# Forty small swap DMAs, a row load of D, and moved buffers in a one-core SSM convolution with an MLP

## The chip, the cores and the metric

The kernel runs on one core of a Trainium2 chip. The metric is the device time of one execution in microseconds (us); the median of the timed runs is compared.

## The reference

Two residual blocks over x of shape 2048 x 640 (bf16). Block A is a gated long convolution: a four-tap causal shift of k, times v, convolved along the sequence with one 2048-tap filter per channel, plus a skip term D. Block B is a Mish MLP of width 1728.

```python
x = A_q
h = x + A_ref(layernorm(x), A_k, A_v, A_shift_k, A_ssm_k, A_ssm_D)
h2 = h + B_ref(layernorm(h), B_w1, B_b1, B_w2)

def A_ref(q, k, v, shift_k, ssm_k, ssm_D):
    kv = causal_shift(k, shift_k) * v            # 4 taps per channel
    y = irfft(rfft(pad(kv)) * rfft(pad(ssm_k)))  # convolution over 2048 steps
    return q * (y + kv * ssm_D)
def B_ref(x, w1, b1, w2):
    h = x @ w1 + b1
    return (h * tanh(softplus(h))) @ w2
```

## The kernel before, in words

The convolution is done as a transform in two matmul stages, a product, and an inverse in two stages. The 640 channels are five blocks of 128 (`dc`), in two groups: group 0 is dc 0 to 2 (96 channel groups of the array `KP`), group 1 is dc 3 and 4 (64).

- **Filter side.** `dadd` adds D to the first filter tap (DVE, L458), `k1pe` transposes the filter (PE, L466), `s1kpe` is stage 1 (PE, L409 and L410), `s2kpe` stage 2 with the table G (PE, L438). The spectrum lands in `KP`.
- **Swap.** The product of complex numbers needs `KP` with its upper and lower 64 partitions exchanged. `swap` copies it to `KPS` by DMA within SBUF (L564): one DMA for each half of each group, four in all.
- **Signal side.** `ktpe` transposes k (L491), `kspe` applies the taps as 76 small matmuls for each dc (L514), `kv` multiplies by v (DVE, L525), then stage 1 (`s1vpe`) and stage 2 (`s2vpe`, L438). ACT evicts stage 2 into a ring `xa`; `prod` multiplies it into `KP` and `KPS` (DVE, L637).
- **Inverse and MLP.** `i1pe` (L648, L649), then for each of 16 row tiles: `i2pe` (L687), the gate `wb` (DVE, L699), the residual `h` (L703), LayerNorm statistics (L708), the scaling `dr` (L717), a transpose `trpe` (L724), the MLP matmuls `m1pe` (L743) and `m2pe` (L759), and the last addition `res` (L768). LayerNorm of x (`ln1`, L596) runs in between.

Evictions out of PSUM have one line for each engine: L316 is ACT, L318 is DVE. PSUM has four double banks (`PS`) in the convolution.

All big arrays are views into one SBUF tile, `arena`, at offsets written out by hand, and share space over time. `KPS` lies over the filter and over k, so it may be written once both have been read. Its part for group 1 also holds `kvb3` and `kvb4`, the kv blocks of dc 3 and 4 (`OFF_KVB2`), so the second swap is issued after `s1vpe3` and `s1vpe4`.

The order on each engine comes from `_schedule`, a list planner in Python with costs and priorities written into the `OP` calls. Each engine then runs its list in order and waits on semaphores. All loads, swaps and stores are issued from SP's queue; the loads of D and of the constants from ACT's; the taps and b1 from POOL's. Eight semaphores serve the DMAs of SP's and ACT's queues in turn, so a DMA is issued once the one eight places ahead of it has landed.

Of the kernel before, what the change touches and what calls it, by code (L numbers as in the profile page):

```python
# [40 lines left out]
OFF_KVB2 = OFF_KPS + 24576  # L41
# [196 lines left out]
def kernel(  # L238
# [90 lines left out]
    Dn = small.tile([P, NDC], BF16, name="Dn")  # L329
# [19 lines left out]
    OP("warm", ("act", 0.2), w=["dumm"], emit=emit_warm, prio=-1)
    def emit_consts(e):  # L350
        nc.scalar.dma_start(consts[:], dram["consts"])
        nc.scalar.dma_start(Dn[:], A_ssm_D.rearrange("(c p) -> p c", p=P))
# [148 lines left out]
    def shift_s(dc, prio):  # L501
# [4 lines left out]
        def ks(e):  # L506
            kvb.tile = view([P, 64, 16, 2], OFF_KVB + dc * 4096 if dc < 3 else OFF_KVB2 + (dc - 3) * 4096)
            outs = [ps_alloc(x).rearrange("p (i t d) -> p i t d", i=2, t=16) for x in rts]
            for src in range(-3, 16):
# [7 lines left out]
                after=wr + ([o for o in ops if o.name.startswith("ktpe")] if dc >= 3 else []))  # L517
# [75 lines left out]
    for t2 in range(16):  # L593
        def fn(e, t2=t2):
            for hh in range(2):
                nc.vector.bn_stats(st1[:, t2, hh, :], xn_t()[:, t2, hh * 320:(hh + 1) * 320])  # L596
            nc.vector.bn_aggr(mv1[:, t2, :], st1[:, t2, :, :])
        OP(f"ln1_{t2}", ("dve", 1.1), r=[("x", t2)], w=[("mv1", t2)], emit=fn, prio=58 if t2 < 4 else CHAIN[t2])
    for lo, hi in ((0, 4), (4, 8), (8, 12), (12, 16)):
        OP(f"ln1s{lo}", ("pool", 1.0), r=[("mv1", t) for t in range(lo, hi)] + ["mhalf"], w=[("r1", t) for t in range(lo, hi)], prio=45,  # L600
           emit=lambda e, lo=lo, hi=hi: rsqrt_eps(r1v[:, lo:hi], mv1[:, lo:hi, 1], hi - lo))

        def ln1f_emit(e, lo=lo, hi=hi):
            nc.vector.scalar_tensor_tensor(nmr1[:, lo:hi], mv1[:, lo:hi, 0], -1.0, r1v[:, lo:hi], ALU.mult, ALU.mult)
        OP(f"ln1f{lo}", ("dve", 0.2), r=[("r1", t) for t in range(lo, hi)], w=[("nmr1", t) for t in range(lo, hi)], emit=ln1f_emit, prio=45)
# [3 lines left out]
    for grp in range(2):  # L609
# [3 lines left out]
        for ci in range(len(ch)):  # L613
            xa = _RT(R_XA, f"xa{grp}_{ci}")
            s1k_pes = [x for x in ops if x.name.startswith("s1kpe")] if (grp, ci) == (0, 0) else []
            rt, o, f0, nf = s2_pe("s2v", grp, ci, lambda grp=grp: B_t[grp]("bvs"), f"bvs{grp}", 25 + grp * 10, xa, s1k_pes)
# [61 lines left out]
    ks_pes = [o for o in ops if o.name.startswith("kspe")]
    for t2 in range(16):
# [38 lines left out]
        o_dr = OP(f"dr{t2}", ("dve", 0.42), r=[("x", t2), ("mv2", t2), ("r2", t2)], allocs=[hc], emit=drf, prio=pr, after=ks_pes)  # L718
# [95 lines left out]
```

## Time and profile before

| | us |
|---|---|
| median of 3 runs | 272.43 (272.22 to 274.0) |
| the profiled execution, its own time | 271.45 |
| span of its instructions | 269.5 |
| PE busy | 223.9 (83%) |
| DVE busy | 155.0 (58%) |
| ACT busy | 138.9 (52%) |

The profiled execution took 1.95 us more than its span, and 0.98 us less than the median of the runs. Busy shares are a mean over stages that differ: the convolution is the first 125 us, and the MLP with its LayerNorms the rest.

### The profile page before, as it was taken

The numbers are of one execution on the slowest core, as the hardware profiler recorded it, in microseconds if no ns is written. First come the engines' busy times: TensorE is split into PE (matmuls) and PEld (weight loads), VectorE is DVE, ScalarE is ACT, GpSimd is POOL, SyncE is SP. The second block draws the span as 40 slices with busy tenths as digits, with TensorE's granted clock in tenths as the row PEclk, the third lists the DMA queues.
The fourth block names the chain that finished last, engine by engine and source line by source line (L and its number), as shares of the span: only waits on it lengthen the run. The fifth ranks groups of instructions, "written<-read, shape, count | busy, mean of one in ns | idle before, by whom it ended". The sixth has DMA issues, their size and how long they took to land.

```text
span 269.5 us, 6850 instructions
## 1 busy us (share of the span) xinstructions
PE 223.9 (83%) x3018; PEld 169.1 (63%) x3024; DVE 155.0 (58%) x300; ACT 138.9 (52%) x192; POOL 22.6 (8%) x56
## 2 busy tenths in 40 slices
PE   2069799885097597894899999999999999999994
PEld 2059788774086497792788774755577557744672
DVE  0038889888069976998899988813862101210121
ACT  2028699284079976975587297445711460056200
POOL 5000000000000000021231132200220000000000
PEclk9999999999569979998699999999999999999999
DMA  6999900029945199960000000010001000100011
GB/s 235 319 416 418 419 19 2 6 61 215 196 150 246 41 202 259 398 233 2 1 2 24 11 18 2 0 49 4 0 24 51 24 0 27 49 24 2 1 47 49
DMA packets 8285, 28.63 MB, mean 106 GB/s; under 512 B 1408, under 2 KB 5312, under 8 KB 6592
## 3 DMA queue, kind: packets, MB, share of 16 engines
q1 hardware_dynamic: 7344, 28.02, 31.4%
q8 instruction: 23, 0.38, 0.6%
q10 hardware_dynamic: 800, 0.17, 0.5%
q0 software_dynamic: 112, 0.01, 0.1%
q14 instruction: 6, 0.05, 0.1%
HBM read 20.33 MB, written 2.62 MB: 85 GB/s over the span
## 4 chain that ended last, share of the span: by engine, by line
PE 57%; DVE 18%; DMA 10%; issue 6%; ACT 5%; POOL 2%; ACTq 0%; DVEq 0%; SPq 0%; POOLq 0%
PE banks L759 23%; PE banks L743 19%; DVE arena L318 6%; DMA Dn<-in_A_ssm_D_dram 5%; DVE arena L637 4%; ACT arena L316 4%; DMA arena<-arena 4%; PE banks L409 4%; DVE st L596 3%; DVE arena L525 3%; PE banks L466 2%; PE banks L438 2%; PE banks L687 2%; PE banks L514 2%; PE banks L724 2%
## 5 line engine op out<-in xcount | busy, mean ns | idle before, releaser
L316 ACT CAST arena<-banks 128x1024 bf16<-128x1024 f32 (+3 forms) x76 | 69.5, 1003 | 27.4 <-PE banks L410 20.8
L749 ACT ACTIVATE arena<-banks,b1s 128x512 bf16<-128x512 f32 (+2 forms) x84 | 43.9, 548 | 46.7 <-PE banks L743 45.5
L743 PE MATMUL banks<-arena 128*128 128x512 bf16 (+2 forms) x414 | 64.4, 311 | 0.9 <-DVE arena L318 0.6
L759 PE MATMUL banks<-arena 128*128 128x320 bf16 x448 | 62.3, 299 | 0.0
L759 PEld LDWEIGHTS <-arena 128*128 128x128 bf16 x448 | 43.6, 98 | 16.8
L743 PEld LDWEIGHTS <-arena 128*128 128x128 bf16 x420 | 36.6, 100 | 24.7 <-issue 0.7
L768 DVE TENSOR_TENSOR arena<-banks,arena 128x640 bf16<-128x640 f32 x16 | 13.1, 818 | 58.7 <-PE banks L759 58.7
L318 DVE CAST arena<-banks 128x1024 bf16<-128x1024 f32 (+1 forms) x28 | 32.8, 1203 | 6.5 <-PE banks L410 4.2
L438 PE MATMUL banks<-arena 128*128 128x64 bf16 (+1 forms) x512 | 23.8, 204 | 5.3 <-ACT arena L316 2.7
L409 PE MATMUL banks<-consts,arena 128*64 128x128 bf16 x320 | 24.7, 234 | 2.3 <-ACT arena L316 1.2
L410 PE MATMUL banks<-consts,arena 128*64 128x128 bf16 x320 | 25.2, 236 | 1.4 <-issue 1.4
L438 PEld LDWEIGHTS <-arena 128*128 128x128 bf16 x512 | 21.4, 101 | 7.6 <-issue 6.7
L637 DVE TENSOR_TENSOR arena<-arena 128x960 bf16<-128x960 bf16 (+2 forms) x42 | 24.4, 661 | 2.5 <-DMA arena<-arena 2.2
L316 ACT COPY arena<-banks 128x1024 bf16<-128x1024 bf16 (+1 forms) x14 | 11.6, 852 | 26.1 <-PE banks L466 15.0
L410 PEld LDWEIGHTS <-arena 128*64 128x64 bf16 x320 | 21.1, 120 | 3.7 <-issue 3.4
L409 PEld LDWEIGHTS <-arena 128*64 128x64 bf16 x320 | 21.6, 120 | 2.5 <-issue 1.5
L648 PE MATMUL banks<-consts,arena 128*128 128x128 bf16 x160 | 19.1, 220 | 2.1 <-DVE arena L637 1.8
L694 ACT ACTIVATE arena<-arena,nmr,r1v 128x640 bf16<-128x640 bf16 x16 | 14.6, 926 | 10.5 <-DVE arena L703 10.2
L466 PE MATMUL banks<-consts,arena 128*128 128x128 bf16 x80 | 7.4, 262 | 14.5 <-DVE arena L458 9.1
L649 PE MATMUL banks<-consts,arena 128*128 128x128 bf16 x160 | 18.9, 221 | 0.6 <-DVE arena L637 0.6
L699 DVE TENSOR_TENSOR arena<-banks,arena 128x384 bf16<-128x384 f32 (+1 forms) x32 | 13.7, 468 | 8.9 <-PE banks L687 8.5
L525 DVE TENSOR_TENSOR arena<-banks,arena 128x512 bf16<-128x512 f32 x20 | 12.4, 682 | 9.2 <-PE banks L514 9.1
(41 smaller groups left out, 180.0 us busy)
## 6 DMA issues: line engine op xcount, KB each, us to landing
arena<-tab_G SPq DMA_DIRECT2D x4, 1024.0 KB, 11.8
arena<-arena SPq DMA_DIRECT2D x2, 1536.0 KB, 13.7
arena<-in_A_ssm_k_dram SPq DMA_DIRECT2D x5, 512.0 KB, 7.8
arena<-in_A_k_dram SPq DMA_DIRECT2D x2, 1280.0 KB, 12.7
arena<-in_A_v_dram SPq DMA_DIRECT2D x2, 1280.0 KB, 16.8
arena<-in_A_q_dram SPq DMA_DIRECT2D x2, 1280.0 KB, 7.7
out_dram<-arena SPq DMA_DIRECT2D x16, 160.0 KB, 1.7
arena<-in_B_w_dram SPq DMA_DIRECT2D x1, 2160.0 KB, 11.0
```

The source lines that it names most:

```text
L316: nc.scalar.copy(o, i)
L318: nc.vector.tensor_copy(o, i)
L409: nc.tensor.matmul(ps1[0:64, gl, :], lhs, fcfs_b[:, 0, :], start=True, stop=True)
L410: nc.tensor.matmul(ps1[64:128, gl, :], lhs, fcfs_b[:, 1, :], start=True, stop=True)
L438: nc.tensor.matmul(ps2[:, c0:c0 + nd], G_t()[:, f0 + fl, :], src[:, f0 + fl, :], start=True, stop=True)
L525: nc.vector.tensor_tensor(kvb.tile[:, q * 16:(q + 1) * 16], rts[h].tile[:, i * 512:(i + 1) * 512].rearrange("p (t d m) -> p d t m", t=16, ...
L637: nc.vector.tensor_tensor(kp, x, kp, ALU.mult)
L648: nc.tensor.matmul(pz[:, gl, :], KP_t()[:, dg, :], a12_b[:, 0, :], start=True, stop=False)
L649: nc.tensor.matmul(pz[:, gl, :], KPS_t()[:, dg, :], a12_b[:, 1, :], start=False, stop=True)
L743: nc.tensor.matmul(ph[:, 0:w], w1_t()[:, dc, fc * P:(fc + 1) * P], lnhT_t()[:, dc, c0:c0 + w], start=(dc == 0), stop=(dc == NDC - 1))
L749: nc.scalar.activation(ub_t[u % 2]()[:, fc, 0:w], rt.tile[:, 0:w], ACT.Mish, bias=b1s[:, fc:fc + 1], scale=1.0)
L759: nc.tensor.matmul(po[:, hf2 * 512:hf2 * 512 + 320], hb[:, fc, tl * P:(tl + 1) * P], w2_t()[:, fc, hf2 * 320:(hf2 + 1) * 320], start=(fc = ...
```

## The change

1. **D as a row.** D is loaded as one row of 640 elements on one partition (`Drow`) and no longer as 640 single elements over 128 partitions (`Dn`). Five one-row matmuls (`drow`) turn it into columns in PSUM, where `dadd` reads it; the bank pair stays taken until the last `dadd`.
2. **Warm-up.** Ten 512-column matmuls on zeros (`pewarm`) stand first on PE, and 4, 6 and 2 more (`kw`) behind `i2pe` of tiles 1, 2 and 3.
3. **Swap in pieces.** Each half and group is copied in pieces of 8 channel groups: 40 DMAs of 64 rows of 2 KB, in place of 4 DMAs with rows of 24 KB and 16 KB. They are sent in the order of the channel groups, both halves of 16 groups in turn. Pieces from group 80 on wait for the transposes of k.
4. **Moved buffers.** `kvb3` and `kvb4` go to the place of the filter transposes (`OFF_KK`), the ring `xa` to the place of `kT` (`OFF_XA = OFF_KT`), the later rings to what is then free, with three slots instead of two. Group 1's swap so no longer has to wait for `s1vpe3` and `s1vpe4`; `kspe` of dc 3 and 4 waits for the filter's stage 1 instead of the transposes of k, and the first `s2vpe` of each group for all `kspe`.
5. **Planner costs** of the LayerNorm helpers are lowered; with the new dependencies and costs the planner orders several engines anew.

```diff
-OFF_KVB2 = OFF_KPS + 24576
+OFF_KVB2 = OFF_KK
+OFF_XA = OFF_KT
...
+    def emit_pewarm(e):
+        pw = ps_alloc(wrt)
+        for i in range(10):
+            nc.tensor.matmul(pw[:, 0:512], warm[:, 0:128], warm[:], start=True, stop=True)
...
-        nc.scalar.dma_start(Dn[:], A_ssm_D.rearrange("(c p) -> p c", p=P))
+        nc.scalar.dma_start(Drow[:], A_ssm_D.rearrange("(o d) -> o d", o=1))
...
+    def emit_drow(e):
+        pd = ps_alloc(drt)
+        for dc in range(NDC):
+            nc.tensor.matmul(pd[:, dc:dc + 1], Drow[:, dc * P:(dc + 1) * P], ident_b[0:1, 0:1], start=True, stop=True)
...
-                after=wr + ([o for o in ops if o.name.startswith("ktpe")] if dc >= 3 else []))
+                after=wr + ([o for o in ops if o.name.startswith("s1kpe")] if dc >= 3 else []))
...
         for half in range(2):
-            def emit_swap(e, half=half, grp=grp):
-                d0, d1 = GRP_DG[grp]
-                a, b = (0, 64) if half == 0 else (64, 0)
-                nc.sync.dma_start(KPS_t()[a:a + 64, d0:d1, :].rearrange("p g f -> p (g f)"),
-                                  KP_t()[b:b + 64, d0:d1, :].rearrange("p g f -> p (g f)"))
-            DMA(f"d_swap{grp}_{half}", 64 * nd * 256, emit_swap, r=[("KP", grp, ci) for ci in range(len(ch))],
-                w=[("KPS", grp, half)], prio=2,
-                after=[o for o in ops if o.name.startswith(("k1pe", "ktpe") + (("s1vpe3", "s1vpe4") if grp else ()))])
+            for g0 in range(GRP_DG[grp][0], GRP_DG[grp][1], 16):
+                def emit_swap(e, half=half, g0=g0):
+                    if not swap_todo:
+                        swap_todo.extend((h, g) for g in range(0, NDG, 16) for h in range(2))
+                    half, g0 = swap_todo.pop(0)
+                    a, b = (0, 64) if half == 0 else (64, 0)
+                    for g1 in (g0, g0 + 8):
+                        nc.sync.dma_start(KPS_t()[a:a + 64, g1:g1 + 8, :].rearrange("p g f -> p (g f)"),
+                                          KP_t()[b:b + 64, g1:g1 + 8, :].rearrange("p g f -> p (g f)"))
+                free = ("k1pe",) + (("ktpe",) if g0 >= 80 else ())
...
+    KW = {1: 4, 2: 6, 3: 2}
...
+        if t2 in KW:
+            krt = _RT(PB, f"kw{t2}")
+            def kwf(e, krt=krt, n=KW[t2]):
+                pw = ps_alloc(krt)
+                for i in range(n):
+                    nc.tensor.matmul(pw[:, 0:512], warm[:, 0:128], warm[:], start=True, stop=True)
+            OP(f"kw{t2}", ("pe", 0.22 * KW[t2]), r=["warm"], allocs=[krt], emit=kwf, prio=pr, after=[o_pe])
```

**The order on SP's queue**, from the load of v on. Before (64x12288 is a half of group 0, 64x8192 one of group 1, `in_A_q` is x):

```order
L384 DMA arena<-in_A_v_dram 128x5120 x2
L564 DMA arena<-arena 64x12288 x2
L587 DMA arena<-in_A_q_dram 128x5120 x2
L564 DMA arena<-arena 64x8192 x2
L590 DMA arena<-tab_t2m 128x4096
L663 DMA arena<-in_B_w_dram 128x5x1728
```

The same place on SP's queue after the change, where L589 is the swap's line:

```order
L403 DMA arena<-in_A_v_dram 128x5120 x2
L589 DMA arena<-arena 64x1024 x40
L613 DMA arena<-in_A_q_dram 128x5120 x2
L616 DMA arena<-tab_t2m 128x4096
L692 DMA arena<-in_B_w_dram 128x5x1728
```

Group 1's swap now stands ahead of the load of x, and x and t2m stand behind all 40 pieces.

**The order on DVE** around the products, before (L525 is `kv`, 128x128x8 an eviction of stage 1, L637 `prod`, 96 for group 0 and 64 for group 1; 128x32x32 an eviction of `i1`):

```order
L525 TENSOR_TENSOR arena<-banks,arena 128x512 x8
L318 CAST arena<-banks 128x128x8
L637 TENSOR_TENSOR arena<-arena 128x96x10 x24
L637 TENSOR_TENSOR arena<-arena 128x96x8 x2
L318 CAST arena<-banks 128x128x8
...
L318 CAST arena<-banks 128x32x32 x2
L637 TENSOR_TENSOR arena<-arena 128x64x16 x16
L318 CAST arena<-banks 128x32x32 x2
```

And after, on DVE at the same place (L544 is `kv`, L319 the eviction, L666 `prod`):

```order
L544 TENSOR_TENSOR arena<-banks,arena 128x512 x8
L319 CAST arena<-banks 128x128x8 x4
L666 TENSOR_TENSOR arena<-arena 128x96x10 x24
L666 TENSOR_TENSOR arena<-arena 128x96x8 x2
L666 TENSOR_TENSOR arena<-arena 128x64x16 x16
L319 CAST arena<-banks 128x32x32 x2
```

The products of group 1 now follow those of group 0 directly, all stage-1 evictions of DVE stand ahead of both, and the LayerNorm and `i1` work that lay between them comes behind. Over the list from the first `dadd` to the first `wb`, DVE has 17 stage-1 casts (13 before), the two casts of one more stage-2 chunk of the filter (96x5 and 96x3), 10 bf16 copies (13 before) and 4 `i1` casts (5 before).

## Rows read from the trace of the kernel before

**Rows 1.** DVE in order of time; in brackets its idle time before, and what ended it.
```profile
15.94 0.23 DVE L458 TENSOR_TENSOR arena<-arena,Dn 128x1 bf16<-128x1 bf16 x2 [15.07 <-DMA Dn<-in_A_ssm_D_dram]
...
74.39 2.48 DVE L525 TENSOR_TENSOR arena<-banks,arena 128x512 bf16<-128x512 f32 x4 [7.90 <-PE banks L514]
78.44 1.22 DVE L318 CAST arena<-banks 128x1024 bf16<-128x1024 f32 x1 [1.56 <-PE banks L410]
79.96 14.69 DVE L637 TENSOR_TENSOR arena<-arena 128x960 bf16<-128x960 bf16 x26 [0.30 <-ACT arena L316]
...
100.17 2.36 DVE L318 CAST arena<-banks 128x1024 bf16<-128x1024 f32 x2 [1.37 <-PE banks L649]
104.76 9.72 DVE L637 TENSOR_TENSOR arena<-arena 128x1024 bf16<-128x1024 bf16 x16 [2.23 <-DMA arena<-arena]
```

**Rows 2.** Busy us by stretch: PE, PEld, DVE, ACT, POOL; granted clock, DMA share, GB/s.
```profile
15.90:64.00 48.10, 43.19 (x1186) 39.14 (x1187) 40.91 (x53) 35.16 (x38) 0.38 (x3) 1.00 0.50 183
...
79.90:104.70 24.80, 19.61 (x384) 17.98 (x384) 21.10 (x38) 22.54 (x27) 0.36 (x1) 0.93 0.64 177
104.70:125.30 20.60, 15.44 (x270) 14.17 (x268) 19.22 (x39) 15.87 (x18) 3.20 (x5) 1.00 0.70 256
125.30:269.50 144.20, 137.08 (x998) 90.14 (x1003) 67.50 (x161) 59.94 (x105) 15.19 (x36) 0.98 0.05 19
```

**Rows 3.** PE in order of time, at the first filter transposes.
```profile
5.28 1.82 PE L466 MATMUL banks<-consts,arena 128*128 128x128 bf16 x15 [5.28 <-DMA arena<-in_A_ssm_k_dram]
16.16 2.04 PE L466 MATMUL banks<-consts,arena 128*128 128x128 bf16 x17 [9.06 <-DVE arena L458]
```

**Rows 4.** The page: DMA issues by tensor, KB of each, us from issue to landing.
```profile
arena<-arena SPq DMA_DIRECT2D x2, 1536.0 KB, 13.7
...
out_dram<-arena SPq DMA_DIRECT2D x16, 160.0 KB, 1.7
...
consts<-tab_consts ACTq DMA_DIRECT2D x1, 168.0 KB, 4.2
...
Dn<-in_A_ssm_D_dram ACTq DMA_DIRECT2D x1, 1.2 KB, 14.7
```

**Rows 5.** The chain that ended last: start us, us, what.
```profile
64.77 8.75 issue
...
93.29 11.37 DMA arena<-arena
...
130.77 3.65 PE banks L743 x45
...
134.70 1.50 PE banks L743 x25
```

**Rows 6.** Busy us in two shorter stretches, columns as in Rows 2.
```profile
20.00:32.00 12.00, 11.30 (x289) 10.46 (x286) 10.96 (x15) 9.80 (x11) 0.00 (x0) 1.00 1.02 422
...
64.00:74.00 10.00, 1.25 (x67) 1.07 (x70) 2.48 (x4) 0.00 (x0) 0.00 (x0) 0.70 0.92 198
```

**Rows 7.** The page: the queue of instruction fetches (packets, MB), and the granted clock in 40 slices.
```profile
PEclk9999999999569979998699999999999999999999
...
q8 instruction: 23, 0.38, 0.6%
```

**Rows 8.** SP's queue in order of time: start us, us, issues.
```profile
0.72 2.90 SPq L369 DMA_DIRECT2D arena<-in_A_ssm_k_dram  x5
...
58.29 3.38 SPq L564 DMA_DIRECT2D arena<-arena  x2
```

**Rows 9.** What SP's queue waited for: us in total, times, longest.
```profile
SPq L564 <- PE banks L410: 15.0, 1, 15.0
SPq L564 <- PE banks L491: 12.4, 1, 12.4
```

**Rows 10.** Groups of DVE instructions by form: count, busy us and mean ns, idle before.
```profile
L318 DVE CAST arena<-banks 128x1024 bf16<-128x1024 f32 x21 | 25.3, 1220 | 6.0 <-PE banks L410 4.2 <-PE banks L649 1.4
...
L318 DVE COPY arena<-banks 128x1024 bf16<-128x1024 bf16 x13 | 8.4, 684 | 2.3 <-PE banks L491 1.3 <-ACT arena L316 0.6 <-PE banks L466 0.4
```

More of the change, by code (lines that the diff above doesn't have):

```diff
@@ L48 @@
 OFF_T2M = OFF_KVB
-OFF_LNX = OFF_KT
-OFF_HC = OFF_KT + 2560
-OFF_OB = OFF_KT + 6400 - 640
+OFF_LNX = OFF_KVB + 8192
+OFF_HC = OFF_KT
+OFF_OB = OFF_KT + 3840
 class _Ring:
@@ L328 @@
     mhalf = small.tile([P, 16], F32, name="mhalf")
-    Dn = small.tile([P, NDC], BF16, name="Dn")
+    Drow = small.tile([1, D], BF16, name="Drow")
+    warm = small.tile([P, 512], BF16, name="warm")
     sk_b = small.tile([P, NDC, 4], BF16, name="sk_b")
@@ L457, in kernel_dc @@
         OP(f"dadd{dc}", ("dve", 0.08), r=["Dn"], w=[("kn", dc)], prio=9,
-           emit=(lambda e: nc.vector.tensor_tensor(kn_t()[:, dc, 0:1], kn_t()[:, dc, 0:1], Dn[:, dc:dc + 1], ALU.add)))
+           emit=(lambda e: nc.vector.tensor_tensor(kn_t()[:, dc, 0:1], kn_t()[:, dc, 0:1], drt.tile[:, dc:dc + 1], ALU.add)), uses=[drt])
         rt = _RT(PS, f"k1_{dc}")
@@ L560, in swap @@
         for half in range(2):
-            def emit_swap(e, half=half, grp=grp):
-                d0, d1 = GRP_DG[grp]
-                a, b = (0, 64) if half == 0 else (64, 0)
-                nc.sync.dma_start(KPS_t()[a:a + 64, d0:d1, :].rearrange("p g f -> p (g f)"),
-                                  KP_t()[b:b + 64, d0:d1, :].rearrange("p g f -> p (g f)"))
-            DMA(f"d_swap{grp}_{half}", 64 * nd * 256, emit_swap, r=[("KP", grp, ci) for ci in range(len(ch))],
-                w=[("KPS", grp, half)], prio=2,
-                after=[o for o in ops if o.name.startswith(("k1pe", "ktpe") + (("s1vpe3", "s1vpe4") if grp else ()))])
+            for g0 in range(GRP_DG[grp][0], GRP_DG[grp][1], 16):
[8 more added lines that the diff above has]
+                free = ("k1pe",) + (("ktpe",) if g0 >= 80 else ())
+                DMA(f"d_swap{grp}_{half}_{g0}", 1.6 * 64 * 4096, emit_swap, r=[("KP", grp, ci) for ci in range(len(ch))],
+                    w=[("KPS", grp, half, g0)], prio=2,
+                    after=[o for o in ops if o.name.startswith(free)])
     swap(0)
@@ L591, with ln1_group, fn, ln1f_emit @@
         after=[o for o in ops if o.name.startswith("s1vpe")])
[L593 to L603, printed above, removed]
+    def ln1_group(lo, hi, prio, after=(), rp=None):
+        for t2 in range(lo, hi):
+            def fn(e, t2=t2):
+                for hh in range(2):
+                    nc.vector.bn_stats(st1[:, t2, hh, :], xn_t()[:, t2, hh * 320:(hh + 1) * 320])
+                nc.vector.bn_aggr(mv1[:, t2, :], st1[:, t2, :, :])
+            OP(f"ln1_{t2}", ("dve", 1.1), r=[("x", t2)], w=[("mv1", t2)], emit=fn, prio=rp[t2 - lo] if rp else prio, after=after)
+        OP(f"ln1s{lo}", ("pool", 0.75), r=[("mv1", t) for t in range(lo, hi)] + ["mhalf"], w=[("r1", t) for t in range(lo, hi)], prio=prio,
+           emit=lambda e: rsqrt_eps(r1v[:, lo:hi], mv1[:, lo:hi, 1], hi - lo))
+        def ln1f_emit(e):
             nc.vector.scalar_tensor_tensor(nmr1[:, lo:hi], mv1[:, lo:hi, 0], -1.0, r1v[:, lo:hi], ALU.mult, ALU.mult)
-        OP(f"ln1f{lo}", ("dve", 0.2), r=[("r1", t) for t in range(lo, hi)], w=[("nmr1", t) for t in range(lo, hi)], emit=ln1f_emit, prio=45)
+        OP(f"ln1f{lo}", ("dve", 0.1), r=[("r1", t) for t in range(lo, hi)], w=[("nmr1", t) for t in range(lo, hi)], emit=ln1f_emit, prio=prio)
+    for lo in (0, 4, 8, 12):
+        ln1_group(lo, lo + 4, 45, rp=[58 if t < 4 else CHAIN[t] for t in range(lo, lo + 4)])
     zb_t = [lambda: big("zbA", [P, 2, 16, 384], OFF_BA), lambda: big("zbB", [P, 2, 16, 256], OFF_BB)]
@@ L614 @@
             xa = _RT(R_XA, f"xa{grp}_{ci}")
-            s1k_pes = [x for x in ops if x.name.startswith("s1kpe")] if (grp, ci) == (0, 0) else []
-            rt, o, f0, nf = s2_pe("s2v", grp, ci, lambda grp=grp: B_t[grp]("bvs"), f"bvs{grp}", 25 + grp * 10, xa, s1k_pes)
+            free = [x for x in ops if x.name.startswith("kspe")] if ci == 0 else []
+            rt, o, f0, nf = s2_pe("s2v", grp, ci, lambda grp=grp: B_t[grp]("bvs"), f"bvs{grp}", 25 + grp * 10, xa, free)
             def e1(e, rt=rt, xa=xa, f0=f0, nf=nf, nd=nd, per=per):
@@ L637, in f2 @@
                     nc.vector.tensor_tensor(kp, x, kp, ALU.mult)
-            prods.append(OP(f"prod{grp}_{ci}", ("dve", 2 * _dve2(nf * nd)), r=[("KPS", grp, 0), ("KPS", grp, 1)],
+            prods.append(OP(f"prod{grp}_{ci}", ("dve", 2 * _dve2(nf * nd)), r=[k for k in last_w if k[0] == "KPS" and k[1] == grp],
                             w=[("KP", grp, ci)], uses=[xa], emit=f2, prio=25 + grp * 10, after=[oe]))
@@ L672 @@
     DMA("d_w2", 2.2e6, emit_w2, w=["w2"], prio=4, after=i1_pes)
-    R_LNX = ring("lnx", 2)
-    R_HC = ring("hc", 2)
-    R_OB = ring("ob", 2)
+    KW = {1: 4, 2: 6, 3: 2}
+    R_LNX = ring("lnx", 3)
+    R_HC = ring("hc", 3)
+    R_OB = ring("ob", 3)
     lnhT_t = lambda: big("lnhT", [P, NDC, S], OFF_LNHT)
-    ks_pes = [o for o in ops if o.name.startswith("kspe")]
+    s1v_pes = [o for o in ops if o.name.startswith("s1vpe")]
+    prod_ops = [o for o in ops if o.name.startswith("prod")]
     for t2 in range(16):
@@ L717, in drf @@
             nc.vector.tensor_scalar(hc.tile, xn_t()[:, t2, :], mv2[:, t2, 0:1], r2[:, t2:t2 + 1], ALU.subtract, ALU.mult)
[L718 removed]
+        o_dr = OP(f"dr{t2}", ("dve", 0.42), r=[("x", t2), ("mv2", t2), ("r2", t2)], allocs=[hc], emit=drf, prio=pr, after=prod_ops)
         rtt = _RT(PB, f"tr_{t2}")
```

14 lines of the change are left out of this document (10 added, 4 removed).

## The prediction

> **What bounds the kernel now.** I read three views first: DVE in order of time, the busy time by stretch, and the chain that ended last. From 125.3 us on, PE is busy 137.08 of 144.20 us [rows 2]: the MLP is a fixed tail of PE work. So the question is how early the first gate multiplication `wb`, which opens that tail, can run; before it is at 125.4 us, right behind the last stretch of [rows 2].
>
> In front of it DVE is the engine to follow. It starts at 15.94 us [rows 1], is busy 40.91 of 48.1 us, 21.10 of 24.8 and 19.22 of 20.6 in the three stretches shown ahead of the tail [rows 2], and stands still in a few long gaps. Look in [rows 1] at the brackets: 15.07 us for the load of D; 7.90 us for `kspe` (L514) and 1.56 us for stage 1 behind it; 1.37 us just before group 1's products and 2.23 us for the second swap. PE waits 9.06 us for the same load of D [rows 3].
>
> The 7.90 us comes from PE: the chain has 8.75 us of "issue" in the middle of 76 equal matmuls [rows 5], a time in which PE waited for nothing that the profile shows, and PE is busy 1.25 of 10 us there [rows 6]. It falls into the first swap, issued at 58.29 us [rows 8], whose two DMAs land 13.7 us after issue [rows 4]. My reading is that PE had no instructions: the 23 fetches of instructions run over the same DMA engines [rows 7], and the swap's rows of 24 KB hold an engine for long. At 198 GB/s over 16 engines [rows 6] a row of 24,576 bytes takes 2.0 us; four are due on each engine in each half. A busy DMA alone does not starve PE: from 20 to 32 us the engines are full at 422 GB/s with rows of 8 and 10 KB (about 0.3 us each by the same division), and PE is busy 11.30 of 12 us [rows 6].
>
> One rule of the Trainium skill speaks against this reading. "Runtime: NRT & Kernel Launch", section "Instruction fetch mechanics", calls the cost of crossing a fetch block "mostly hidden". If that held here, the 8.75 us would have another cause and could stay; the first rival below has the price. The trace does not bear the rule out in this stretch, since nothing else explains the pause.
>
> **The change, part by part.** Times are of the profiled execution, 271.45 us.
>
> (a) D as a row, −9.7 us. The 640 elements landed 14.7 us after issue; the constants, 168 KB on the same queue just ahead, in 4.2 us [rows 4]. One row of 1,280 bytes behind them should land about 1 us after them. Issued at about 1.1 us, that is between 5.3 us (the constants' own 4.2) and 15.8 us (as before). I take 6, since its form is nearer to the constants. The first filter tile is there at 5.28 us [rows 3]. So `dadd`, at 15.94 before, runs at about 6.2: 9.7 us earlier. Behind it, DVE and ACT evict all five filter blocks as before. The ten warm-up matmuls lie in PE's wait for that load and cost nothing: 15 transposes of 128 columns took 1.82 us there [rows 3], so ten matmuls of four times the columns are some 4.9 us (an estimate), from about 1.1 to 6.0. Bounds −10.3 to 0.
>
> (b) No pause in `kspe`, −9.5 us. With rows of 2 KB an engine is held 2,048 / (198/16 GB/s) = 0.17 us at a time, less than the 0.3 us at which PE was not starved. The DVE gaps of 7.90 and 1.56 us go [rows 1]. What is late next? The products need group 0's part of `KPS`, the first 24 pieces. The swap's wait for `ktpe` (L491, 12.4 us before 58.29 [rows 8, 9]) falls away for the first pieces, so they could have been issued at 45.9 us; with (a) and some 2.4 us for the new order of stage 2, that is 38.6. A piece is 131 KB, at 198 GB/s 0.66 us; SP's issue costs 2.90 / 5 = 0.58 us each [rows 8], so the transfer sets the pace. Group 0 is complete at 38.6 + 1.2 + 24 x 0.66 = 55.6, all 40 pieces at 66.2. DVE comes to its products at 79.96 − 9.7 − 9.5 + the 5 stage-1 casts moved ahead of them (5 x 1.22 = 6.1, less 2.8 of cheaper work elsewhere) = about 64. Slack is 8 us. Bounds −9.5 to 0.
>
> (c) Group 1 no longer waits, −3.6 us. Its swap waited 15.0 us for the last stage 1 of the signal (L410) [rows 9] and took 11.37 us on the chain [rows 5]. Now it is complete at 66.2, and DVE comes to group 1's products at 64 + 14.69 = 78.7, 12 us later. The gaps of 1.37 and 2.23 us [rows 1] close, as DVE has work queued without a break. Bounds −3.6 to 0. x and t2m stand behind all pieces on SP and are issued at about 60 us, when the last eight are under way; x is first read after both sets of products, at about 88 us. That is no cost.
>
> (d) DVE's own list, +2.8 us. Four more stage-1 casts at 1.22 (+4.9), the two casts of the extra chunk, at most one more cast (+1.2), three copies fewer at 0.68 (−2.0), one `i1` cast fewer (−1.2) [rows 10]. DVE is the busy engine here, so these count in full. Bounds 0 to +2.8, as ACT gives up what DVE takes.
>
> (e) Clock at the start of the MLP, −0.5 us. The granted clock is at 0.6 there [rows 7]: 45 small MLP matmuls take 3.65 us, 25 later ones 1.50 [rows 5], so 45 at full clock would take 2.7: 0.95 us to gain if `kw` keeps PE at its 2.4 GHz. But `kw` adds 12 matmuls of 512 columns in PE's waits for `wb`: by four times the 128-column price, 12 x 4 x 0.060 = 2.9 us at full clock and 12 x 4 x 0.12 = 5.8 us at the price of [rows 3]. Some of it may show. Bounds −1 to +2.
>
> The buffers with three slots add no instruction, and `kspe` of dc 3 and 4 waits for a stage done long before: nothing.
>
> Sum: −9.7 − 9.5 − 3.6 + 2.8 − 0.5 = **−20.5 us**. 271.45 − 20.5 = 250.95; the median of the runs stood 0.98 above the profiled execution, so **251.9 us**. A cross-check: DVE's busy time from 15.9 us to `wb` is 40.91 + 21.10 + 19.22 [rows 2] and 2.48 + 2.48 + 1.22 between them [rows 1, 6], 87.4 us, and its gaps are 22; without 13.1 us of gaps, with 2.8 more work and a start at 6.2, `wb` comes at 6.2 + 87.4 + 2.8 + 8.9 = 105.3, 20 us earlier.
>
> **The rivals.**
>
> The pause comes back (0.14). PE's fetches wait behind the swap whatever its rows are. For: the pieces now keep the engines busy for some 27 us instead of 2 x 8. Against: PE ran through 12 us of full engines [rows 6]. It would cost the 8.75 us again: about 260.5.
>
> DVE's other gaps close too (0.14). In the stretch to 64 us DVE has 7.2 us of idle time [rows 2], partly from PE at the low clock at the start. With PE warm from the first transposes half of it and (d) could go, −3.6 and −2.8: about 245.5.
>
> The change doesn't do what it says for D (0.04): a row on one partition lands as late as the 640 elements. (a) is gone, 261.6.
>
> Pieces somewhat slow (0.06): at 1.2 us each instead of 0.66, all 40 end at 39.8 + 48 = 87.8, 9 us after DVE wants them: about 261.
>
> Slower (0.04). The forty DMAs do not overlap: each pays its landing. The nearest row is the store of 160 KB, which lands in 1.7 us when alone [rows 4]. Then the last piece lands at 39.8 + 40 x 1.7 = 107.8, and group 1's products start 3.0 us later than the 104.76 before; all the rest follows as before, with (e): about 275. The point from which it decides: at 251.9 the products have 78.7 us to wait for, and 20.5 us more brings the old time back, which is (78.7 + 20.5 − 39.8) / 40 = 1.5 us a piece. Against it: eight DMAs may be in flight at once, and the five filter loads were issued 0.58 us apart [rows 8] and ran at the rates of full engines.
>
> The Trainium skill has a rule for this side. "DMA: Bandwidth & Descriptors", section "Rules for kernel authors", asks for at least 1 MiB a DMA and warns that small ones are mostly overhead; its section "Bandwidth" lists 0.95 us for 64 KB and 6.15 us for 1 MB, from which an estimate for 131 KB one after another is 1.3 us, and the sum would then be about 265. No row here shows DMAs of this size within SBUF.
>
> **How the numbers follow.** The forecast has 0.58, and the rivals the rest. A measurement of this kernel tells about 1% (2.7 us) from no change. The range reaches from 245 (the second rival) to 262 (the pause, slow pieces, D late); the slower rival and pieces slower still are outside. Faster by over 1%: 0.94; within 1%: 0.02; slower by over 1%: 0.04, the slower rival alone. The 0.02 are pieces near 1.5 us, out of the 0.06 above.
>
> **What would show it.** (a) DVE's first `dadd` at about 6 us. (b) No "issue" of several us at the line of `kspe`; 40 pieces within some 27 us from about 39 on; the products start near 64. (c) No DMA ahead of group 1's products, which follow group 0's without a gap. (d) `wb` at about 103 to 105. (e) The granted clock near 1 at the first MLP matmuls. The forecast is wrong if the products wait for a DMA, if PE's pause moves elsewhere, or if ACT, which alone evicts the signal's stage 2, holds DVE back now that the swap doesn't.

## The result, and the profile after

The changed kernel takes **250.69 us** (median of 12 runs, 249.66 to 251.79) against 272.43 before: a ratio of 0.926, 95% interval 0.922 to 0.930. The forecast was 251.9, so the time was met within 1.2 us. The profiled execution took 249.66 us, its span 247.9, 21.6 less than before; the gain lies wholly ahead of the MLP, as the first two views show.

DVE in order of time, in the kernel after (L477 is `dadd`, L666 `prod`, L738 `wb`); the rows answer to [rows 1]:

```profile
5.70 0.16 DVE L477 TENSOR_TENSOR arena<-arena,banks 128x1 bf16<-128x1 bf16 x1 [4.56 <-PE banks L383]
...
59.76 4.64 DVE L319 CAST arena<-banks 128x1024 bf16<-128x1024 f32 x4
64.32 23.10 DVE L666 TENSOR_TENSOR arena<-arena 128x960 bf16<-128x960 bf16 x40
...
103.72 0.84 DVE L738 TENSOR_TENSOR arena<-banks,arena 128x384 bf16<-128x384 f32 x2
```

The first `dadd` comes 10.2 us earlier, the products start 15.6 us earlier, and 40 of the 42 products of both groups run as one block, right behind the four stage-1 casts that were moved ahead of them: there is no bracket in front of it, so DVE waited for no DMA. The gate `wb` comes 21.7 us earlier. From the start of the products to `wb` it is 39.4 us, and 45.4 before.

Busy time by stretch in the kernel after, columns as in [rows 2]:

```profile
5.70:64.30 58.60, 51.00 (x1496) 46.68 (x1497) 52.09 (x66) 44.13 (x47) 0.38 (x3) 1.00 0.77 254
64.30:87.80 23.50, 17.05 (x277) 15.52 (x276) 23.12 (x41) 18.56 (x22) 0.36 (x1) 0.78 0.91 305
78.60:101.50 22.90, 22.12 (x385) 21.62 (x386) 20.66 (x42) 20.11 (x22) 2.29 (x4) 0.93 0.74 265
87.80:103.70 15.90, 14.91 (x252) 14.32 (x251) 13.96 (x31) 14.99 (x17) 1.92 (x3) 1.00 0.49 162
103.70:247.90 144.20, 137.69 (x1010) 89.47 (x1014) 68.22 (x166) 57.96 (x104) 16.54 (x38) 0.99 0.06 19
```

Three things are to be seen. The tail is as long as before, 144.20 us. From the first `dadd` to `wb`, 98.0 us, DVE is busy 52.09 + 23.12 + 13.96 = 89.2 us and idle 8.8. And from 78.6 us on PE is busy 22.12 of 22.9 us with the signal's stage 2 and `i1`: PE now seems to bound the last stretch ahead of `wb`; experiment 7 tries that. In the stretch of the products its granted clock is 0.78.

PE in order of time at the last two `kspe` (L533) of the kernel after, where before had its 8.75 us:

```profile
53.73 2.22 PE L533 MATMUL banks<-diagm,arena 32*128 32x32 bf16 x152
55.89 0.70 PE L457 MATMUL banks<-arena 128*128 128x96 bf16 x10
```

All 152 matmuls run without a pause. The swap in the meantime: first SP's queue in order of time, in three stretches, then the page's row of the issues.

```profile
40.27 31.51 SPq L589 DMA_DIRECT2D arena<-arena  x40
...
41.59 2.53 SPq L589 DMA_DIRECT2D arena<-arena  x4
...
43.52 2.15 SPq L589 DMA_DIRECT2D arena<-arena  x2
```
```profile
q8 instruction: 24, 0.39, 0.6%
...
arena<-arena SPq DMA_DIRECT2D x40, 128.0 KB, 3.2
```

Four issues in a row take 0.63 us each; two of which one meets an instruction fetch, at 44.2 us, take 2.15. Six of the 24 fetches fall between the pieces, and at each one issue of SP, and one piece on the engines, is 0.6 to 1.2 us longer, 5.8 us of issues in all. That is how 40 pieces took 31.5 us to issue.

The clock, page line of the kernel after:

```profile
PEclk9999999999957899999999999999999999999998
```

The dip now lies in the products' stretch. There PE had run from 65.5 us on in bursts of ten matmuls with pauses of 1.2 and 0.55 us, waiting for ACT to evict; then the trace has it at 1.2 GHz from 69.0 to 75.8 us. From 72.4 on it ran without pauses, and from 75.8 it is at 2.4 GHz. It stood still from 76.3 to 78.6, is at 1.2 GHz from 79.2 to 82.6, ran on, and is at 2.4 GHz from there. The MLP starts at 2.4 GHz, where before had 0.6 of it [rows 7]. PE's first MLP matmuls in the kernel after, against 3.65 us for the same 45 in [rows 5]:

```profile
109.66 2.67 PE L782 MATMUL banks<-arena 128*128 128x128 bf16 x45 [0.15 <-DVE arena L319]
```

### The profile page after: what moved, and what is told of

It reads as the page before. It is cut to its first block, busy times and chain, and to the rows that moved or that the text cites. A ratio compares the mean times of both kernels' runs of the same rounds, so it can differ in the third digit from the quotient of the medians.

```text
span 247.9 us, 6995 instructions
## 1 busy us (share of the span) xinstructions
PE 224.7 (91%) x3044; PEld 167.6 (68%) x3051; DVE 157.7 (64%) x304; ACT 137.1 (55%) x189; POOL 22.7 (9%) x56
## 4 chain that ended last, share of the span: by engine, by line
PE 63%; DVE 22%; DMA 5%; issue 3%; POOL 2%; ACT 2%; SPq 1%; DVEq 0%; ACTq 0%; POOLq 0%
PE banks L798 23%; PE banks L782 19%; DVE arena L666 6%; DVE arena L319 4%; PE banks L678 4%; PE banks L677 4%; PE banks L457 3%; DMA arena<-in_A_ssm_k_dram 3%; DVE arena L544 3%; PE banks L428 3%; DVE st L747 2%; DVE st L623 2%; PE banks L763 2%; ACT arena L317 2%; PE banks L533 2%
## 5 line engine op out<-in xcount | busy, mean ns | idle before, releaser
L317 ACT CAST arena<-banks 128x1024 bf16<-128x1024 f32 (+2 forms) x71 | 66.4, 1001 | 14.5 <-PE banks L457 3.8
L788 ACT ACTIVATE arena<-banks,b1s 128x512 bf16<-128x512 f32 (+2 forms) x84 | 43.2, 545 | 46.3 <-PE banks L782 45.5
L782 PE MATMUL banks<-arena 128*128 128x512 bf16 (+2 forms) x414 | 63.3, 307 | 0.5 <-DVE arena L319 0.2
L798 PEld LDWEIGHTS <-arena 128*128 128x128 bf16 x448 | 43.6, 98 | 16.8
L782 PEld LDWEIGHTS <-arena 128*128 128x128 bf16 x420 | 35.4, 98 | 24.4 <-issue 0.4
L319 DVE CAST arena<-banks 128x1024 bf16<-128x1024 f32 (+3 forms) x33 | 37.3, 1167 | 3.6 <-PE banks L457 1.3
L457 PE MATMUL banks<-arena 128*128 128x96 bf16 (+1 forms) x512 | 25.3, 210 | 6.8 <-ACT arena L317 3.9
L457 PEld LDWEIGHTS <-arena 128*128 128x128 bf16 x512 | 22.9, 104 | 9.0 <-issue 8.7
L317 ACT COPY arena<-banks 128x1024 bf16<-128x1024 bf16 (+1 forms) x16 | 13.8, 894 | 21.7 <-PE banks L763 13.4
L666 DVE TENSOR_TENSOR arena<-arena 128x960 bf16<-128x960 bf16 (+2 forms) x42 | 24.4, 656 | 0.4 <-ACT arena L317 0.4
L428 PE MATMUL banks<-consts,arena 128*64 128x128 bf16 x320 | 21.2, 219 | 3.4 <-DVE arena L319 1.5
L677 PE MATMUL banks<-consts,arena 128*128 128x128 bf16 x160 | 19.9, 226 | 2.6 <-DVE arena L666 2.3
L429 PEld LDWEIGHTS <-arena 128*64 128x64 bf16 x320 | 18.4, 110 | 5.0 <-issue 4.5
L429 PE MATMUL banks<-consts,arena 128*64 128x128 bf16 x320 | 21.6, 221 | 0.0
L678 PE MATMUL banks<-consts,arena 128*128 128x128 bf16 x160 | 19.7, 226 | 0.2 <-DVE arena L666 0.2
L428 PEld LDWEIGHTS <-arena 128*64 128x64 bf16 x320 | 18.7, 109 | 0.6
L738 DVE TENSOR_TENSOR arena<-banks,arena 128x384 bf16<-128x384 f32 (+1 forms) x32 | 13.6, 465 | 8.6 <-PE banks L718 8.5
L677 PEld LDWEIGHTS <-arena 128*128 128x128 bf16 x160 | 16.2, 102 | 2.4 <-DVE arena L666 2.4
L678 PEld LDWEIGHTS <-arena 128*128 128x128 bf16 x160 | 16.2, 102 | 0.9 <-issue 0.5
```

The lines of the kernel that those rows point to most:

```text
L317: nc.scalar.copy(o, i)
L319: nc.vector.tensor_copy(o, i)
L428: nc.tensor.matmul(ps1[0:64, gl, :], lhs, fcfs_b[:, 0, :], start=True, stop=True)
L429: nc.tensor.matmul(ps1[64:128, gl, :], lhs, fcfs_b[:, 1, :], start=True, stop=True)
L666: nc.vector.tensor_tensor(kp, x, kp, ALU.mult)
L677: nc.tensor.matmul(pz[:, gl, :], KP_t()[:, dg, :], a12_b[:, 0, :], start=True, stop=False)
```

## The experiments

Ratios are against the kernel before, run on the same chip; losses are against the 250.69 us of the change. Experiments 5 to 8 ran on a chip on which before took 271.46 us, and the change itself was not run there, so differences of a microsecond are read from the traces and not from the medians. Each kernel differs from the changed one, or from before, by the diff that it shows; experiment 11 is the change again.

**1. D as elements again.** The load of D goes back to 640 elements, the one-row matmuls are left out, all else is the change.

```diff
-        nc.scalar.dma_start(Drow[:], A_ssm_D.rearrange("(o d) -> o d", o=1))
+        nc.scalar.dma_start(Dn[:], A_ssm_D.rearrange("(c p) -> p c", p=P))
```

> The changed kernel with D loaded again as 640 single elements; its five one-row matmuls are left out, everything else and the order as changed. Theory: term (a) is the load alone. The first addition of D comes at 15 to 16 us instead of 5.7, DVE shows a gap of some 9 us there, and the time rises by 9 to 10 us to about 260. Rival: filter loads and the warm clock carry part of the gain, so the loss is under 5 us (below 256).

Measured: 259.61 us, ratio 0.954 (0.948 to 0.960), a loss of 8.9 us. DVE in order of time shows the first `dadd` (L475 here) back at its old place:

```profile
16.10 0.23 DVE L475 TENSOR_TENSOR arena<-arena,Dn 128x1 bf16<-128x1 bf16 x2 [14.97 <-DMA Dn<-in_A_ssm_D_dram]
```

From the products to `wb` it is 39.2 us, 39.4 in the change, so the loss lies ahead of them. (a) is worth 8.9 us in the presence of the rest, against 9.7 forecast.

**2. The kernel before with rows of 2 KB.** Each of the four swaps is cut into two DMAs of alternating 2 KB blocks; place, order and amount stay.

```diff
-                nc.sync.dma_start(KPS_t()[a:a + 64, d0:d1, :].rearrange("p g f -> p (g f)"),
-                                  KP_t()[b:b + 64, d0:d1, :].rearrange("p g f -> p (g f)"))
+                for odd in range(2):
+                    cut = lambda t, r: t[r:r + 64, d0:d1, :].rearrange("p (n o e) f -> p o n (e f)", o=2, e=8)[:, odd]
+                    nc.sync.dma_start(cut(KPS_t(), a), cut(KP_t(), b))
```

> The kernel before, with each swap DMA cut into two that take every other 2 KB of a row; same bytes, same place on the queue, rows of 2 KB instead of 24 and 16 KB. Theory: PE starves for instructions behind long rows. The 8.75 us of issue in kspe falls below 1 us. DVE then reaches the products near 70.5 us, but the first swap still lands at about 75.5, so only 4 to 9 us come back: 264 to 268. Rival: a busy DMA queue starves PE whatever the rows: the pause stays at 7 us or more and the time at 272.

> The kernel before with swap rows of 2 KB once more, for a profile at the usual clock. As expected there: by the theory no pause of over 1 us in kspe, DVE at the products near 70.5 us but held by the swap until about 75.5, time 264 to 268; by the rival the pause is there.

Measured: 267.88 us, ratio 0.982 (0.976 to 0.989), with one execution of four, the profiled one, at 572.33 us; and 266.74 in a single execution later, from which the trace is. What PE waited for there (line, releaser, us in total, times, longest; L514 is `kspe`):

```profile
PE banks L514 <- issue: 5.0, 1, 5.0
```

The pause shrinks from 8.75 to 5.0 us and does not go, and another of 1.3 us follows at stage 2. With rows of 2 KB, as short as those of the change, PE was still out of instructions for 5 us. The length of a row is therefore not what decides it, and the reason given in (b) is not sufficient.

**3. The change with four large swaps.** The same buffers and order, but one DMA for each half and group, sent when the last piece of `KPS` is free.

```diff
+                    if g0 not in (80, 96):
+                        return
                     a, b = (0, 64) if half == 0 else (64, 0)
-                    for g1 in (g0, g0 + 8):
+                    d0, d1 = (0, 96) if g0 == 80 else (96, 160)
...
```

> The changed kernel with four large swap DMAs again (rows of 24 and 16 KB), group 0's pair issued where the pieces from group 80 on stand, behind the last transposes of k, group 1's right behind it. Theory: long rows starve PE. A pause of 4 to 8 us shows on PE between 56 and 70 us with nothing waited for, group 0 lands near 67 instead of 62, and the time is 254 to 260. Rival: the pause was due to something else in the old order: no pause over 2 us, only the later landing, 252 to 254.

Measured: 266.94 us, ratio 0.980 (0.975 to 0.986), a loss of 16.3 us: more than either theory had. PE in order of time:

```profile
63.74 1.90 PE L533 MATMUL banks<-diagm,arena 32*128 32x32 bf16 x76 [8.12 <-issue]
...
74.32 0.32 PE L428 MATMUL banks<-consts,arena 128*64 128x128 bf16 x1 [3.74 <-issue]
...
83.26 0.94 PE L457 MATMUL banks<-arena 128*128 128x96 bf16 x18 [2.90 <-issue]
```

The pause comes back, three times, for 14.8 us in all, now that all four swaps stand behind one another. DVE stands still for 7.53 and 6.70 us behind the first two, and its products start at 80.48 us, 16.2 later, with 39.4 us from there to `wb` as in the change: that is the whole loss. The third comes when DVE has its products to do and costs nothing. The rest of the change is all there, so it was the cutting of the swap, and the earlier start that goes with it (40.3 us against 50.1), that removed the pause.

**4. The buffers back.** `kvb3`, `kvb4` and the ring `xa` return to their old places, and group 1's pieces wait again for `s1vpe3` and `s1vpe4`.

```diff
-OFF_KVB2 = OFF_KK
+OFF_KVB2 = OFF_KPS + 24576
-OFF_XA = OFF_KT
+OFF_XA = OFF_KK
...
-                after=wr + ([o for o in ops if o.name.startswith("s1kpe")] if dc >= 3 else []))
+                after=wr + ([o for o in ops if o.name.startswith(("s1kpe", "ktpe"))] if dc >= 3 else []))
...
-                free = ("k1pe",) + (("ktpe",) if g0 >= 80 else ())
+                free = ("k1pe",) + (("ktpe",) if g0 >= 80 else ()) + (("s1vpe3", "s1vpe4") if g0 >= 96 else ())
```

> The changed kernel with kvb3, kvb4 and the ring xa at their old places, so group 1's pieces wait for the last stage 1 of the signal again (the planner then puts group 1's products behind LayerNorm and i1 work). Theory: term (c), 3.6 us: gaps before group 1's products come back, 253 to 255. Rival: with the pause gone and group 0's products later, group 1's pieces land in time anyway: within 1 us of 250.7.

Measured: 255.98 us, ratio 0.939 (0.932 to 0.946), a loss of 5.3 us. DVE in order of time:

```profile
63.64 14.69 DVE L666 TENSOR_TENSOR arena<-arena 128x960 bf16<-128x960 bf16 x26 [3.90 <-DMA arena<-arena]
...
88.87 9.72 DVE L666 TENSOR_TENSOR arena<-arena 128x1024 bf16<-128x1024 bf16 x16 [0.16 <-issue]
```

Group 1's products start about 10 us later than in the change (64.32 + 14.69 = 79.0), since the planner has put LayerNorm and eviction work between the groups. They wait for no DMA: the bracket has 0.16 us, and the gaps that the theory expected ahead of them do not come back. In so far the rival was right; in the time it was not. The products of group 0 wait 3.9 us for their pieces here, since the planner's new order lets DVE come to them at 59.7 us, 4.6 earlier than in the change. So the 5.3 us are what the moved buffers and the order that the planner makes with them are worth together; the experiment doesn't part the two, and it doesn't measure (c).

**5. No warm-up at the start.** The ten `pewarm` matmuls are left out.

```diff
-        for i in range(10):
-            nc.tensor.matmul(pw[:, 0:512], warm[:, 0:128], warm[:], start=True, stop=True)
```

> The changed kernel without the ten warm-up matmuls at the start (they compute nothing that is used). Theory: they lie in the wait for D and the first stage is bound by DVE and ACT, so they are worth 0 to 1.5 us: 250.7 to 252. Rival: starting PE at the low clock delays the whole filter stage: over 2 us, 253 or more.

Measured: 251.3 us (250.48 to 252.24), ratio 0.926 (0.922 to 0.930). No difference that the measurement can tell.

**6. No matmuls behind `i2pe`.**

```diff
-    KW = {1: 4, 2: 6, 3: 2}
+    KW = {}
```

> The changed kernel without the 12 filler matmuls behind the first i2 tiles (nothing uses them). Theory: term (e), they keep the full clock for the first MLP matmuls; without them the granted clock falls there and 0.5 to 2 us are lost: 251 to 253. Rival: they cost more than they bring: 249 to 250.5.

Measured: 252.93 us (251.22 to 253.78), ratio 0.931 (0.926 to 0.936). PE in order of time at the first MLP matmuls, beside 2.67 us for 45 in the change:

```profile
111.85 4.37 PE L782 MATMUL banks<-arena 128*128 128x128 bf16 x42 [0.58 <-DVE arena L319]
```

From `wb` to the end this kernel takes 145.95 us and the change 144.20, so `kw` saves 1.75 us there: without it PE is at 1.2 GHz from 109.0 to 115.8 us. `wb` itself also came 1.9 us later in this profile, with no `kw` ahead of it. That comes from ahead of the products, which start at 66.25 us here, 1.9 later than in the change, and have the same 39.4 us to `wb`; PE stood still for 1.4 us at 21 us and for 1.0 at the last `kspe`. The other profiles have products between 64.65 and 65.68 us (experiments 11, 5 and 7), so this part seems to vary from run to run. The medians have 2.2 us in all.

**7. PE kept busy in the products.** The one dip that the change has left is in the stretch of the products, so matmuls on zeros go there too.

```diff
+            if xa is not None and grp == 0 and (ci >= 5 or ci == 0):
+                for _ in range(2):
+                    nc.tensor.matmul(ps2[:, 0:512], warm[:, 0:128], warm[:], start=True, stop=True)
             for fl in range(nf):
...
+                if d0 == 0 and gi == 0:
+                    for _ in range(6):
+                        nc.tensor.matmul(pz[:, 0:512], warm[:, 0:128], warm[:], start=True, stop=True)
```

> The changed kernel with filler matmuls also during group 0's products: two of 512 columns ahead of each later chunk of stage 2 and six ahead of the first i1 tile, into the bank that the real matmuls then overwrite. Theory: from 78.6 to 101.5 us PE bounds the way to the first wb, and its first 32 i1 matmuls run at the low clock (94 to 98 ns apart against 56): 1 to 2 us come back, 248.7 to 249.7. Rival: DVE still bounds that stretch, or the fillers delay stage 2: 250.5 or more.

Measured: **249.25 us** (248.37 to 249.48), ratio 0.918 (0.914 to 0.922). Each of its six runs lies below each of the 12 of the change. The page's clock, and DVE in order of time (L669 is `prod`, L745 `wb`):

```profile
PEclk9999999999999999999999999999999999999998
```
```profile
65.68 24.32 DVE L669 TENSOR_TENSOR arena<-arena 128x960 bf16<-128x960 bf16 x42
...
103.48 0.84 DVE L745 TENSOR_TENSOR arena<-banks,arena 128x384 bf16<-128x384 f32 x2
```

From the start of the products to `wb` it takes 37.8 us, and the change 39.4; its repeat and experiments 1, 3, 5, 6 and 8, with no edit in that stretch, take 39.2 to 39.4 too. So the 1.6 us stand clear of the spread between runs, and fit PE being the bound there. This is the fastest version of the study.

**8 and 9. Fewer, longer pieces.** Ten DMAs with rows of 8 KB, and twenty with rows of 4 KB, in place of forty with 2 KB. The order, the buffers and the total stay. Of the first:

```diff
-                    for g1 in (g0, g0 + 8):
-                        nc.sync.dma_start(KPS_t()[a:a + 64, g1:g1 + 8, :].rearrange("p g f -> p (g f)"),
+                    if g0 % 32:
+                        nc.sync.dma_start(KPS_t()[a:a + 64, g0 - 16:g0 + 16, :].rearrange("p g f -> p (g f)"),
...
```

> The changed kernel with ten swap DMAs of 32 channel groups, rows of 8 KB (0.6 us each on an engine) instead of 2 KB. Theory: a fetch of PE's instructions waits for about four rows, 2.5 us, which PE's stock covers: no pause over 1 us, 250 to 252. Rival: any row much longer than 2 KB starves PE: a pause of 3 us or more, 254 or more.

> The changed kernel with 20 swap DMAs of 16 channel groups: rows of 4 KB, and 16 KB of each DMA on each engine (1.3 us) instead of 8 KB. By now three theories of PE's pause stand: (P) a fetch waits for one DMA's share on an engine; (R) for some rows; (Q) for all that is queued. P: a wait of about 1.3 us, a pause in kspe of 0 to 1.8 us, 250 to 253. R: about the same. Q: eight DMAs of 1.3 us pile up to 10 us, a pause of 5 us or more, 256 or more.

Measured: 259.99 us, ratio 0.958 (0.953 to 0.963), with 8 KB; 257.72 us, ratio 0.945 (0.939 to 0.950), with 4 KB. PE's waits with 4 KB:

```profile
PE banks L533 <- issue: 4.1, 1, 4.1
...
PE banks L457 <- issue: 2.6, 2, 1.8
PE banks L428 <- issue: 2.5, 1, 2.5
```

With 8 KB there is one of 3.8 us in stage 1, and one of 2.9 at `kspe` that the trace puts down to DVE, though it stands at the same place as the pause of before. The profiled execution with 4 KB took 260.3 us, near the upper end of its runs (256.4 to 261.5), so its pauses may be longer than usual; its fastest run is still 4.6 us above the slowest of the change. Rows of 4 KB take 0.28 us, less than the 0.3 at which (b) took PE to be safe, and still PE paused three times. Two ideas fall here: that the length of a row decides, and that what one DMA puts on one engine decides (four rows of 4 KB are 1.1 us). What differs from the change is how far SP's queue runs ahead. The time from issue to landing of the swap's DMAs (us: least, median, most), the forty pieces first, then the twenty and the ten:

```profile
DMA to landing us min/median/max: 2.3/3.2/4.1
```
```profile
DMA to landing us min/median/max: 3.1/7.0/8.9
```
```profile
DMA to landing us min/median/max: 5.1/8.2/11.7
```

A small piece is issued every 0.65 us between fetches and moves in about as long, so little gathers on the queue. A piece of 4 KB rows is issued every 0.9 us and takes 1.12 us to move; its landing time grows from piece to piece.

**10. The kernel before, one row on each engine.** Each of its swap DMAs is cut in four, of 16 partitions each.

```diff
+                for r in range(0, 64, 16):
+                    nc.sync.dma_start(KPS_t()[a + r:a + r + 16, d0:d1, :].rearrange("p g f -> p (g f)"),
+                                      KP_t()[b + r:b + r + 16, d0:d1, :].rearrange("p g f -> p (g f)"))
```

> The kernel before, each swap DMA cut into four of 16 partitions: rows stay 24 and 16 KB long, but each DMA has one row on each engine (24 KB, 1.9 us) instead of four. P (one DMA's share): the pause in kspe falls from 8.75 us to 1.5 to 3.5. R (length of rows) and Q (all that is queued): the pause stays at 7 us or more. By P the products start near 76 us, where the swap lands, and the time is 264 to 268; by R and Q 271 to 273.

Measured: 288.86 us, ratio 1.060 (1.053 to 1.067): slower than before by 16.4 us. What PE waited for:

```profile
PE banks L438 <- issue: 6.4, 1, 6.4
...
PE banks L514 <- issue: 4.6, 1, 4.6
```

The pause at `kspe` (L514) shrank to 4.6 us, between what P and what R and Q had, and one of 6.4 us came at stage 2. Neither decides the time: DVE waits longer, for the swap. DVE in order of time, at the two groups' products:

```profile
88.80 14.69 DVE L638 TENSOR_TENSOR arena<-arena 128x960 bf16<-128x960 bf16 x26 [13.25 <-DMA arena<-arena]
...
122.47 3.10 DVE L638 TENSOR_TENSOR arena<-arena 128x1024 bf16<-128x1024 bf16 x5 [12.39 <-DMA arena<-arena]
```

A row of 24 KB took 3.23 us (mean of 128) where it took 1.85 in before. So this kernel says little of the price of a pause, and something of how this copy should be cut: not by partitions.

**11. The change again**, beside 9 and 10, with no edit.

> The changed kernel unaltered, on the chip of the two runs beside it, as their measure: 250 to 251.5 by every theory.

Measured: 250.65 us (249.79 to 251.38), ratio 0.921 (0.917 to 0.925).

## Why the prediction was right, point by point

**(a) D, −9.7: shown.** `dadd` at 5.70 us against the 6.2 forecast; undone, it costs 8.9 us (experiment 1).

**(b) No pause, −9.5: the effect shown, the size about right, the reason wrong.** The products start at 64.32 us, as forecast. The pause is PE without instructions, as the prediction read it. Counted over PE's records in the trace, PE stopped after the same record, the 2,497th, in before and in experiments 2, 3, 8, 9 and 10, though their lists differ. Their other pauses stand at 2,241, 2,753, 3,009 and 3,521. All of these are a multiple of 256 apart, and so is every "issue" pause of more than 0.6 us ahead of the MLP in all traces of the study. A fetch is 16 KB (0.39 MB in 24), and there is one to about 255 records: so PE stops at the end of a fetched page. The fetches' own times in the trace show the rest. While PE works on one page, the next one is fetched. For the page that starts behind record 2,241 it went like this:

| kernel | fetch starts, us after PE enters the page | PE's pause at its end, us |
|---|---|---|
| the change | 0.6 | none |
| the change again (11) | 0.8 | 0.5 |
| 8 (rows of 8 KB) | 3.5 | 2.9 |
| 10 (before, by partitions) | 3.6 | 4.6 |
| 2 (before, rows of 2 KB) | 4.9 | 5.0 |
| 9 (rows of 4 KB) | 6.2 | 4.1 |
| before | 8.2 | 8.75 |
| 3 (four large swaps) | 8.7 | 8.1 |

In each kernel with a pause of 2.9 us or more here, PE goes on 1.3 to 1.7 us after that fetch has moved. So a late fetch is the cause, and the swap makes it late: in before the two fetches ahead of the swap start 0.6 and 0.7 us after their page is entered.

What the prediction had wrong is why it is late: rows of 24 KB that hold an engine for long. Rows of 2 KB in the order of before left 5.0 us of the pause, and rows of 4 KB in the order of the change brought 6.6 us of it (4.1 and 2.5). What goes along with the long pauses in all of these kernels is a queue of swap DMAs that runs ahead of the engines: median issue to landing 7.0 us and more in the six that pause (18.2 in experiment 3, 10.8 in before, 7.6 in experiment 2), 3.2 in the change. So short rows alone would not have done it. The pieces helped because SP can't issue them faster than they move, which the prediction did not name as the reason: that (b) came out was in part luck.

The prediction's other ground was that from 20 to 32 us the engines are full of loads and PE runs on [rows 6]. That holds only nearly. In before the fetches at 24.1 and 30.3 us start 3.1 and 3.9 us after PE enters the page, and the chain has a pause at record 705, also a page's end:

```profile
31.54 1.35 issue
```

Loads from DRAM thus make fetches late too, and the change keeps two such pauses, 1.3 and 0.7 us, at records 961 and 1,217, ahead of the swap. In before PE takes about 5 us for a page there, and 2.1 for the one that ends in `kspe`, so a delay costs it less. Why a fetch waits for some of the queued copies and not for all stays open; no run parts this.

The Trainium skill ("Runtime: NRT & Kernel Launch", section "Instruction fetch mechanics") has the crossing of a fetch block "mostly hidden". The runs agree with it for the change in the stretch of the swap (none, and 0.5 us in its repeat), and not for the six kernels with a deep queue, among them before with 8.75 us.

The transfer's pace of 0.66 us a piece was right between the fetches (0.63), the first piece was issued at 40.3 us and not at 38.6, and the prediction left out the six fetches of 0.6 to 1.2 us. The last piece landed at 73.5, forecast 66.2; the 24th had moved at 61.2 and its semaphore came at 63.1, forecast 55.6. Of the 8 us of slack 1.2 were left, and the products, at 64.32, waited for none. x, behind the pieces, was issued at 71.9 us and not at 60, at no cost: its first use is at 92.0.

The same skill's rule of at least 1 MiB a DMA ("DMA: Bandwidth & Descriptors", section "Rules for kernel authors") is given there for bandwidth, and the measured times here go the other way: 128 KB pieces give 250.7 us, 256 KB 257.7, 512 KB 260.0, and the large ones 266.9. Between fetches the small pieces lost no bandwidth: 131 KB in 0.64 us are 205 GB/s, against 198 in before.

**(c) Group 1, −3.6: the gaps closed, the price not measured by itself.** In the trace of the change group 1's products follow group 0's without a wait for a DMA. From the products to `wb` DVE's idle time fell from 5.1 to 2.3 us: the gaps of 1.37 and 2.23 went, and 0.8 us came elsewhere. Experiment 4 undoes the buffers and costs 5.3 us, but by another order on DVE and a wait of group 0.

**(d) DVE's list, +2.8: +1.8.** DVE is busy 89.2 us from the first `dadd` to `wb`, 87.4 before. The sum left out that one LayerNorm of a row tile less stands ahead of `wb` (8 in place of 9, 1.1 us each). DVE's idle time there is 8.8 us, 8.9 forecast.

**(e) Clock, −0.5: 0 on balance.** The 45 matmuls take 2.67 us, as forecast for full clock, 1.0 less than before, yet the tail is 144.20 us in both kernels. Half of the 1.0 is lost ahead of them: the first MLP matmul comes 5.9 us behind `wb`, 5.4 before. What took it and the rest back was not tried; `kw`'s own matmuls stand there, and so does the LayerNorm of (d). Without `kw` the tail would be 1.75 us longer than before's (experiment 6).

**The rivals.** The pause came back, but only in kernels with fewer, larger DMAs. The DMAs did not pay their landing one by one: they land in 3.2 us and follow each other every 0.65 between fetches. The second rival, DVE's other gaps closing with PE warm from the start, did not come: DVE is idle 6.5 us up to the products, and the warm-up at the start is worth nothing that shows (experiment 5). What a low clock cost was later, in the products' stretch: 1.4 us by the medians, 1.6 by the traces (experiment 7).

## What to carry to other kernels

Look for "issue" pauses in PE's chain while a large copy within SBUF is queued. Here they were PE out of instructions: count PE's records between two of them, and see whether they lie a multiple of 256 apart. Cutting the copy until SP issued no faster than it moved ended the long ones here. A short row was not enough, and a cut by partitions made the copy itself slow. Where a wait for data is removed, see which engine is full next: here PE, whose clock then repaid a few matmuls on zeros.

## What the runs showed of the hardware that was not expected

- PE ran dry at the ends of pages of 256 instructions, for 1.3 to 8.75 us at a time, with swap DMAs whose median landing time was 7 us or more, and for 0.7 to 1.35 us under loads from DRAM (before, at 31.5 us; the change, at 27.0 and 33.5). The fetch of the next page had started up to 8.7 us after PE entered the page, in place of 0.6.
- At each of six instruction fetches the piece under way, and SP's issue, took 0.6 to 1.2 us longer: two issues took 2.15 us in place of 1.3.
- A copy within SBUF over 64 partitions moved rows of 24 KB in 1.85 us each, and over 16 partitions at a time in 3.23.
